# Score chunks of an attention pair issued together, the third one in borrowed PSUM banks

## The chip, the cores and the metric

The kernel runs on one core of a Trainium2 chip. The metric is device microseconds for one execution; lower is better. The engines are TensorE (PE: matmuls, and PEld for its weight loads), VectorE (DVE), ScalarE (ACT), GpSimd (POOL) and SyncE (SP), which issues most DMAs. Each engine takes its instructions in the order in which they were written; they are tied together by semaphores.

## The reference: what is computed

Two stages. First an attention with 4 batches, 8 heads, 768 positions and head size 64, in which a query sees the first 8 keys and the 96 before it, with a bias by distance:

```
scores = scale * q @ k.T                       # per head
keep = is_global | is_local                    # first 8 keys, or 0 <= rel < 96
scores = where(keep, scores - slope[h] * dist, -1e9)
x = softmax(scores) @ v                        # heads side by side: [4, 768, 512]
```

Then a mixer on x, with a low rank product over positions (U: 768x32, V: 32x768) and a feed-forward layer of 512 to 2048 to 512:

```
u = x + (x.T @ U @ V).T
out = u + relu(u @ w_ch1) @ w_ch2
```

## The kernel before, in words

**Pairs.** Work goes by pairs of heads: 16 pairs, `i` from 0 to 15, four to a batch (`NP` is 4, `NPE` is 8). Since the window is narrow, a pair's scores take 1408 columns per head instead of 768 x 6: for each of six key blocks a diagonal piece and, for five of them, a piece for the next block. The columns are made in three chunks, `c` = 0, 1, 2, of 512, 512 and 384 columns per head.

**A chunk** (`scores`, L347). Small matmuls with 64 contraction rows, one head in the upper and one in the lower half of the array: 8 for a full chunk, 6 for the third. From pair 4 on they go to `ps_sc()`, a PSUM tile of two banks (one per head) of which there is a single one. `s_dve` (L399) takes it from there: one VectorE operation on both heads multiplies, adds the bias table and writes the SBUF tile `sp` ("bias step" in what follows). `sp` has one buffer. `st_S` is one chunk and its bias step. When all three chunks are in `sp`, `st_E` makes the exp of one head on ScalarE (L415), first head 0, then head 1, into `ep`.

**Around it.** `st_V(i, hi)` multiplies the exp of one head with v into `ps_ob()`, a single bank, and normalises on VectorE (reciprocal L437, product L451); POOL casts the result to fp16 (`x16`, L454). `st_M1` (L457) is x^T U on PE into the same single bank `ps_ob()`; ScalarE copies it (L467); `st_MT` (L477) transposes that on PE (L480) and VectorE copies it (L481); `st_M3` (L511) multiplies with V into `ps_sc()`, VectorE adds it to x (L522) and POOL casts x again (L525). `st_X` sends it through a DMA transpose to `uT`. `st_K` makes the key tile `kA` of the next pair on ScalarE (L339) and VectorE (L340).

**Feed-forward units.** Meanwhile the feed-forward layer of an earlier batch runs in units. An up unit (L631) is 8 matmuls into one bank `ps_th("hps")`, of which there are three in turn, and a relu on ScalarE (L636) that frees it. Down units (L666 for batch 0, L684 for the others, with sums of halves on VectorE, L555, so that seven products stand for eight) go to `ps_cps`, two banks in turn; VectorE adds each to x (L689).

**What sets the order.** The whole program is written out by hand under `manual_schedule`. The main loop (L804) runs over pairs: iteration `i` makes the scores and exps of pair `i`, the v products of pair `i - 1` and its mixer steps. Between these steps stand nine calls `fill(n)`, each of which issues `n` units (up or down, by a rule in `unit`) and, after each unit, VectorE sums that are due. The number of units at the nine places for pairs 7 to 15 is 1, 1, 1, 2, 1, 1, 1, 1, 1. So the order of one iteration before is:

```
S(i,0) u V(i-1,0) u S(i,1) u V(i-1,1) u u S(i,2) u M1(i-1)
E(i,0) u MT(i-1) K(i+1) u M3(i-1) E(i,1) u X(i-1) u
```

where u is a unit. On PE alone S, V, M1, MT, M3 and u are issued; on ScalarE E, K, the copy after M1 and the relus; on VectorE the bias steps, normalisations, additions and sums.

Of the kernel before, what the change touches and what calls it, by code (L numbers as in the profile page):

```python
# [16 lines left out]
ALU = mybir.AluOpType  # L17
# [3 lines left out]
def kernel(  # L21
# [13 lines left out]
    nc = tc.nc  # L35
# [10 lines left out]
    NP = H // 2  # L46
    NPE = 2 * NP
    qk_scale = 1.0 / math.sqrt(D)
# [5 lines left out]
    slope = [2.0 ** (-8.0 * (h + 1) / H) for h in range(H)]  # L54
# [25 lines left out]
    def ps_sc():  # L80

        return psum.tile([P, 2, 512], FP32, name="sc", tag="sc", bufs=1)

    def ps_ob():
        return psum.tile([P, 512], FP32, name="ob", tag="ob", bufs=1)

    def ps_cps(name):
        return psum.tile([P, 512], FP32, name=name, tag="cps", bufs=2)
# [43 lines left out]
    def load_v(i):  # L132
        b, h0 = i // NP, 2 * (i % NP)
        st = stp.tile([P, 2 * NSB, D], FP32, name="vst", tag="vst", bufs=2)
        nc.sync.dma_start(
            st, v[b, h0:h0 + 2].rearrange("h (n p) d -> p (h n) d", p=P)
        )
        vsts[i] = st
# [27 lines left out]
    def warm(n):  # L166
# [13 lines left out]
        out=relB, in_=relB, compare_op=ALU.is_ge, fill=BIG,  # L180
# [3 lines left out]
        out=relB, in_=relB, compare_op=ALU.is_ge, fill=BIG,  # L184
# [50 lines left out]
    def new_batch(b):  # L235
        xs[b] = xp.tile([P, NSB, DM], FP32, name="x_sb", tag="x_sb", bufs=3)
        tmps[b] = xp.tile([P, DM], FP16, name="tmp16", tag="tmp16", bufs=3)
        uTs[b] = xp.tile([P, NDC, S], FP16, name="uT", tag="uT")
# [76 lines left out]
    def st_P(i):  # L315
        nc.vector.tensor_copy(  # L316
            vas[i][0:NG, 1:].rearrange("p n h d -> p n (h d)"),
            vts[i][0:NG, 0:1].rearrange("p n h d -> p n (h d)").broadcast_to(
                (NG, NSB - 2, 2 * (D + 1))
            ),  # L320
        )
# [22 lines left out]

    sps, eps, later = {}, {}, []

    def scores(i, c, on_pe):  # L347

        kT, kA, qT = kts[i], kas[i], qts[i]
        c0 = 512 * c  # L350
        tot = min(512, W - c0)
        r0 = 256 if c else 0
        both = None if on_pe and (i + c) % 2 else ps_sc()
        scs = [ps_cps("sc") if both is None else both[:, hi] for hi in range(2)]
        if on_pe:
            for hi in range(2):
                nc.tensor.matmul(
                    scs[hi][:, 0:tot], slI[:, 2 * (i % NP) + hi],
                    rel16.rearrange("p a c -> p (a c)")[:, r0:r0 + tot], start=True, stop=False,
                )  # L360
        for kb in (2 * c, 2 * c + 1):
            o = 256 * kb - c0
            for hi in range(2):
                r = slice(hi * D, (hi + 1) * D)
                nc.tensor.matmul(  # L365
                    scs[hi][:, o:o + P], kT[r, kb * P:(kb + 1) * P], qT[r, kb * P:(kb + 1) * P],
                    start=(o == 0 and not on_pe), stop=(o + P == tot),
                )
            if kb < NSB - 1:
                for hi in range(2):  # L370
                    r = slice(hi * D, (hi + 1) * D)
                    nc.tensor.matmul(  # L372
                        scs[hi][:, o + P:o + 2 * P], kA[r, kb], qT[r, (kb + 1) * P:(kb + 2) * P],
                        start=False, stop=(o + 2 * P == tot),
                    )
        return scs, both, c0, tot
# [20 lines left out]
    relfs = (relcat2[:, :, 0:512], relcat2[:, :, 256:768], relcat2[:, :, 256:640])  # L397

    def s_dve(i, got):  # L399
        _, both, c0, tot = got  # L400
        if c0 == 0:
            sps[i] = scp.tile([P, 2, W], FP32, name="sp", tag="sp", bufs=1)
        nc.vector.scalar_tensor_tensor(  # L403
            out=sps[i][:, :, c0:c0 + tot], in0=both[:, :, 0:tot],
            scalar=qk_scale / slope[2 * (i % NP)], in1=relfs[c0 // 512],
            op0=ALU.mult, op1=ALU.add,
        )

    def st_S(i, c):
        s_dve(i, scores(i, c, False))  # L410

    def st_E(i, hi):
        if hi == 0:
            eps[i] = scp.tile([P, 2, W], FP16, name="ep", tag="ep")
        nc.scalar.activation(  # L415
            eps[i][:, hi], sps[i][:, hi], AF.Exp, scale=slope[2 * (i % NP)]
        )
# [59 lines left out]
    def st_MT(i):  # L477
        b, dc = i // NP, i % NP
        tps = ps_ob()
        nc.tensor.matmul(tps[:, 0:P], turn16[i % 2], ident16, start=True, stop=True)  # L480
        nc.vector.tensor_copy(tmps[b][:, dc * P:(dc + 1) * P], tps[:, 0:P])  # L481
# [234 lines left out]
    def fill(n):  # L716
        for _ in range(n):
            unit()
            count[0] += 1
            for _ in range(2 if len(jobs) > 4 else 1):  # L720
                for queue in (jobs, slow):
                    if queue and queue[0][0] < count[0]:
                        queue.popleft()[1]()
                        break

    def unit():
        down = downs_q and not held[0] and not any(place(w) <= place(downs_q[0][1]) for _, w in ups_q)
        room = ups_q and (not downs_q or place(ups_q[0][1]) - place(downs_q[0][1])
                          < (3 if held[0] else 2))
        if down and (ahead[0] > 0 or not room):  # L730
            ahead[0] = 0
            downs_q.popleft()[0]()
        elif room:
            ahead[0] = 1
            ups_q.popleft()[0]()
# [68 lines left out]
    for i in range(NP, NPAIR + 2):  # L804
        b, hp = divmod(i, NP)
        live = i < NPAIR
        units = iter(
            (0, 1, 1, 2, 1, 1, 1, 1, 1) if i == NP
            else (0, 1, 1, 1, 1, 1, 1, 1, 1) if i + 1 < NPE
            else (1, 1, 1, 2, 1, 1, 1, 1, 1)  # L810
        )
        held[0] = i < NP + 3
        if hp == 0 and live and b + 1 < B:
            new_batch(b + 1)
        if live and i > NP:
            st_S(i, 0)
        if NPE <= i + 1 < NPAIR:
            turn(i + 1)
        if i + 1 < NPAIR and i != NP + 2:
            load_v(i + 1)  # L820
        if i + 2 < NPE:
            load_qk(i + 2)
        fill(next(units))
        if NPE + 2 <= i + 2 < NPAIR:
            cast_one(i + 2, 1, nc.scalar)
        if NP < i <= NPAIR:
            st_V(i - 1, 0)
        if i == NP:
            load_w1(2)
        if i + 1 < NPE:  # L830
            st_T(i + 1)
        if i == NP:
            load_w1(3)
        fill(next(units))
        if live:
            st_S(i, 1)
        fill(next(units))
        if NP < i <= NPAIR:
            st_V(i - 1, 1)
        if live:  # L840
            cast_v(i)
            st_A(i)
        if NPE + 2 <= i + 2 < NPAIR:
            cast_one(i + 2, 0, nc.scalar)
        if NPE <= i + 3 < NPAIR and i != NP + 2:
            load_qk(i + 3)
        if i > NP + 1 and (i - 2) % NP == NP - 1:
            queue_ff((i - 2) // NP)
            ahead[0] = 1
        if i == NPAIR + 1:  # L850
            break
        fill(next(units))
        if live:
            st_S(i, 2)
        fill(next(units))
        if i > NP:
            st_M1(i - 1)
        else:
            for xo, o, rb in later:
                nc.vector.tensor_tensor(xo, o, rb, ALU.mult)  # L860
        if i == NP + 1:
            load_w2(0)
            load_w2(1)
        if i + 2 < NPE:
            cast_qk(i + 2, nc.gpsimd)
        if i == NP + 1:
            load_w2(2)
            load_w2(3)
        if live:
            st_E(i, 0)  # L870
            if i < NPE:
                st_P(i)
        fill(next(units))
        if i >= NPE:
            for _ in range(min(2, len(kept))):
                kept.popleft()()
        if i > NP:
            st_MT(i - 1)
        if NPE <= i + 1 < NPAIR:
            st_K(i + 1)  # L880
        fill(next(units))
        if i > NP:
            st_M3(i - 1)
        if live:
            st_E(i, 1)
        fill(next(units))
        if i == NP + 1:
            load_v(i + 2)
            load_qk(i + 4)
        if i > NP:  # L890
            st_X(i - 1)
        if NPE <= i + 2 < NPE + 2:
            cast_qk(i + 2, nc.gpsimd)
        fill(next(units))
# [38 lines left out]
```

## Time and profile before

| what | value |
|---|---|
| median of 3 runs | 232.99 us (231.74 to 235.61) |
| the profiled execution, its own time | 231.74 us |
| its span, first to last instruction | 230.0 us |
| granted TensorE clock | 1.00 |
| instructions | 5877 |
| busy: PE, PEld | 220.7, 171.1 us |
| busy: DVE, ACT, POOL | 161.5, 125.8, 72.3 us |
| bias steps, 36 (L403) | 40.7 us on DVE; 1215 ns for 2 x 512 columns, 944 for 2 x 384 |
| exps, 24 (L415) | 33.1 us on ACT, 1380 ns each |
| first score matmul of pairs 7, 8, ... 15 | 61.02, 73.32, 84.85, 96.42, 107.99, 119.19, 130.38, 142.04, 153.24 us |
| last score matmul of pair 15 starts | 159.2 us |

How to read it: the time is that of an execution with what lies around it; the span is from the first to the last instruction of the program. Busy time on PE is modelled from starts, since matmuls overlap in a pipeline: a matmul of 256 columns is printed with some 270 ns, and eight of them follow each other every 109 ns. The distance of starts therefore says more than the printed lengths. VectorE and ScalarE instructions also overlap slightly: the next one starts some 0.08 us before the printed end of the one before. In the group view, "idle before" is the time for which the engine stood before instructions of that group, and the name behind the arrow is what ended most of it.

### The profile page before, as it was taken

How to read it: one execution, taken by the hardware profiler on the slowest of the kernel's cores; microseconds unless marked ns; L12 is line 12 of the kernel's file. 1: busy time of each engine (PE TensorE's matmuls, PEld its weight loads, DVE VectorE, ACT ScalarE, POOL GpSimd, SP SyncE). 2: the span in 40 equal slices, each digit the busy share in tenths (PEclk: the TensorE clock that was granted, in tenths of full speed). 3: DMA queues.
4: the chain of work that ended last, by engine and by line, in shares of the span. 5: the costliest groups of instructions: out<-in, count | busy, mean ns of one | idle time of the engine just before them, and what ended most of it. 6: DMA issues, size and time to landing. Idle time of an engine off the chain costs nothing.

```text
span 230.0 us, 5877 instructions
## 1 busy us (share of the span) xinstructions
PE 220.7 (96%) x2418; PEld 171.1 (74%) x2420; DVE 161.5 (70%) x337; ACT 125.8 (55%) x196; POOL 72.3 (31%) x115
## 2 busy tenths in 40 slices
PE   7989899999999999999999999999999999999993
PEld 2456568788745445888888878888988888888882
DVE  3799876749577979597989897989764444444452
ACT  6787747786805253968485847292732433333320
POOL 6499708297553323123313131313111000000000
PEclk9999999999999999999999999999999999999999
DMA  6999996979999879897979994951321202010022
GB/s 185 335 283 281 281 291 90 321 135 180 191 163 206 201 180 228 203 239 175 261 202 219 242 200 102 144 158 25 88 69 36 94 0 94 0 67 27 10 84 93
DMA packets 86563, 36.68 MB, mean 160 GB/s; under 512 B 74152, under 2 KB 83592, under 8 KB 86536
## 3 DMA queue, kind: packets, MB, share of 16 engines
q1 hardware_dynamic: 81480, 32.01, 57.5%
q0 software_dynamic: 5056, 4.29, 12.4%
q8 instruction: 19, 0.31, 0.6%
q14 instruction: 8, 0.07, 0.1%
HBM read 27.46 MB, written 6.29 MB: 147 GB/s over the span
## 4 chain that ended last, share of the span: by engine, by line
PE 67%; DVE 15%; DMA 7%; ACT 4%; POOL 2%; issue 1%; SPq 0%; ACTq 0%
PE hps L631 25%; PE cx L684 13%; PE cy L684 10%; PE cps L666 8%; DMA w<-in_moe_w_ch_dram 6%; DVE sp L403 3%; PE sc L365 2%; ACT ep L415 2%; DVE x_sb L451 2%; PE tp L254 2%; PE ob L432 2%; DMA kst<-in_k_dram 2%; PE sc L517 1%; PE ob L428 1%; DVE s L555 1%
## 5 line engine op out<-in xcount | busy, mean ns | idle before, releaser
L631 PE MATMUL hps<-uT,w 128*128 128x256 f16 x756 | 96.0, 273 | 0.0
L636 ACT ACTIVATE htr<-hps 128x512 f16<-128x512 f32 x96 | 56.4, 598 | 58.0 <-PE hps L631 57.9
L631 PEld LDWEIGHTS <-w 128*128 128x128 f16 x756 | 70.5, 98 | 9.9 <-issue 0.2
L403 DVE SCALAR_TENSOR_TENSOR sp<-sc,relcat 128x1024 f32<-128x1024 f32 (+1 forms) x36 | 40.7, 1131 | 9.1 <-ACT ep L415 4.8
L415 ACT ACTIVATE ep<-sp 128x1408 f16<-128x1408 f32 x24 | 33.1, 1380 | 0.7 <-DVE sp L403 0.6
L684 PEld LDWEIGHTS <-htr 128*128 128x128 f16 x288 | 27.5, 98 | 3.6
L454 POOL CAST x<-x_sb 128x384 f16<-128x384 f32 x27 | 14.5, 538 | 49.8 <-DVE x_sb L451 45.7
L689 DVE TENSOR_TENSOR x_sb<-cx,x_sb 128x256 f32<-128x256 f32 x36 | 15.2, 422 | 18.3 <-PE cx L684 17.7
L666 PE MATMUL cps<-w,htr 128*128 128x512 f16 x96 | 24.0, 379 | 0.4 <-DMA w<-in_moe_w_ch_dram 0.4
L525 POOL CAST x<-x_sb 128x768 f16<-128x768 f32 x12 | 11.0, 916 | 40.8 <-DVE x_sb L522 40.8
L684 PEld LDWEIGHTS <-s 128*128 128x128 f16 x216 | 20.2, 98 | 2.9 <-DVE s L555 0.6
L689 DVE TENSOR_TENSOR x_sb<-cy,x_sb 128x256 f32<-128x256 f32 x27 | 11.4, 423 | 12.5 <-PE cy L684 12.3
L365 PEld LDWEIGHTS <-kT 64*128 64x128 f16 x192 | 8.3, 93 | 13.7 <-issue 12.4
L451 DVE TENSOR_TENSOR x_sb<-ob,rcp 128x384 f32<-128x384 f32 x30 | 16.7, 558 | 1.0
L365 PE MATMUL sc<-qT,kT 64*128 64x128 f16 x192 | 16.8, 221 | 0.3 <-DVE x_sb L522 0.2
L432 PE MATMUL ob<-v,ep 128*128 128x65 f16 x192 | 16.4, 193 | 0.0
L432 PEld LDWEIGHTS <-ep 128*128 128x128 f16 x192 | 13.8, 98 | 3.1 <-ACT x L787 0.7
L428 PE MATMUL ob<-vA,ep 128*128 128x65 f16 x160 | 14.5, 194 | 1.2 <-DVE vA L316 1.2
L142 POOL CAST v<-vst 128x768 f16<-128x768 f32 x16 | 14.0, 877 | 2.9 <-DMA vst<-in_v_dram 2.9
L372 PE MATMUL sc<-qT,kA 64*128 64x128 f16 x160 | 14.3, 217 | 0.6 <-DVE kA L290 0.4
L666 PEld LDWEIGHTS <-htr 128*128 128x128 f16 x96 | 8.4, 97 | 8.5 <-issue 0.5
L522 DVE TENSOR_TENSOR x_sb<-sc,x_sb 128x768 f32<-128x768 f32 x12 | 11.5, 956 | 4.6 <-PE sc L517 4.6
(109 smaller groups left out, 315.0 us busy)
## 6 DMA issues: line engine op xcount, KB each, us to landing
qst<-in_q_dram SPq DMA_DIRECT2D x16, 384.0 KB, 4.7
kst<-in_k_dram SPq DMA_DIRECT2D x16, 384.0 KB, 6.1
vst<-in_v_dram SPq DMA_DIRECT2D x16, 384.0 KB, 4.0
out_dram<-x_sb SPq DMA_DIRECT2D x23, 256.0 KB, 3.1
w<-in_moe_w_ch_dram POOLq DMA_DIRECT2D x8, 512.0 KB, 8.1
vA<-v SPq DMA_DIRECT2D x8, 152.3 KB, 3.0
out_dram<-x_sb SPq DMA_DIRECT2D x2, 128.0 KB
uT<-x SPq DMA_TRANSPOSE x12, 3.1
```

The lines of the kernel that those rows point to most:

```text
L365: nc.tensor.matmul(scs[hi][:, o:o + P], kT[r, kb * P:(kb + 1) * P], qT[r, kb * P:(kb + 1) * P], start=(o == 0 and not on_pe), stop=(o + P ...
L403: nc.vector.scalar_tensor_tensor(out=sps[i][:, :, c0:c0 + tot], in0=both[:, :, 0:tot], scalar=qk_scale / slope[2 * (i % NP)], in1=relfs[c0 ...
L415: nc.scalar.activation(eps[i][:, hi], sps[i][:, hi], AF.Exp, scale=slope[2 * (i % NP)])
L428: nc.tensor.matmul(ob[:, qi], ep[:, OF[qi - 1]:OF[qi - 1] + P], vA[:, qi - 1, hi], start=True, stop=False,)
L432: nc.tensor.matmul(ob[:, qi], ep[:, DG[qi]:DG[qi] + P], vt[:, qi, hi], start=(qi == 0), stop=True,)
L451: nc.vector.tensor_tensor(xo, ob[:, :, 0:D], rb, ALU.mult)
L454: nc.gpsimd.tensor_copy(x16, xo)
L631: nc.tensor.matmul(hps[:, k * FT:(k + 1) * FT], w1_16[:, dc, jt * P:(jt + 1) * P], uT[:, dc, ts], start=(dc == 0 and k == 0), stop=(dc == ...
L636: nc.scalar.activation(cell["htr"][:, 2 * jp:2 * jp + 2].rearrange("p j t -> p (j t)"), hps, AF.Relu)
L666: nc.tensor.matmul(cps, htr[:, jc, t * P:(t + 1) * P], w2_16[:, jc], start=(b > 0 and jc == 0), stop=(jc == NJC - 1),)
L684: nc.tensor.matmul(ps, cell[a][:, j], weight(w, j), start=(first and j == 0), stop=(done is not None and j == HJ - 1), skip_group_check=True,)
L689: nc.vector.tensor_tensor(x_sb[:, n, cs], ps, x_sb[:, n, cs], ALU.add)
```

## The change

From pair 7 on (`joined = i >= NPE - 1`):

- The third chunk's matmuls are issued right behind the second's (`st_S12`), where the second stood before.
- The third chunk goes to two banks of `ps_th`, the three that the up units and the transposes of q and k take in turn, instead of the one two-bank tile `ps_sc()`. Since these two banks are separate tiles, its bias step is two operations, one per head, of 128 x 384.
- On VectorE the two bias steps of the third chunk stand first, then that of the second chunk.
- The exp of head 0 stands where the third chunk stood (ahead of a unit and M1); the exp of head 1 stands behind MT and ahead of the next pair's `kA` copy, a unit and M3.

```diff
-    def scores(i, c, on_pe):
+    def scores(i, c, on_pe, apart=False):
...
-        both = None if on_pe and (i + c) % 2 else ps_sc()
-        scs = [ps_cps("sc") if both is None else both[:, hi] for hi in range(2)]
+        both = None if apart or on_pe and (i + c) % 2 else ps_sc()
+        bank = ps_th if apart else ps_cps
+        scs = [bank("sc") if both is None else both[:, hi] for hi in range(2)]
...
     def s_dve(i, got):
-        _, both, c0, tot = got
+        scs, both, c0, tot = got
         if c0 == 0:
             sps[i] = scp.tile([P, 2, W], FP32, name="sp", tag="sp", bufs=1)
+        if both is None:
+            for hi, sc in enumerate(scs):
+                nc.vector.scalar_tensor_tensor(
+                    out=sps[i][:, hi, c0:c0 + tot], in0=sc[:, 0:tot],
+                    scalar=qk_scale / slope[2 * (i % NP)], in1=relfs[c0 // 512][:, hi],
+                    op0=ALU.mult, op1=ALU.add,
+                )
+            return
...
+    def st_S12(i):
+
+        mid = scores(i, 1, False)
+        s_dve(i, scores(i, 2, False, True))
+        s_dve(i, mid)
...
         fill(next(units))
+        joined = i >= NPE - 1
         if live:
-            st_S(i, 1)
+            st_S12(i) if joined else st_S(i, 1)
         fill(next(units))
...
         fill(next(units))
-        if live:
+        if live and joined:
+            st_E(i, 0)
+        elif live:
             st_S(i, 2)
         fill(next(units))
         if i > NP:
...
-        if live:
+        if live and not joined:
             st_E(i, 0)
-            if i < NPE:
-                st_P(i)
+        if live and i < NPE:
+            st_P(i)
         fill(next(units))
...
         if i > NP:
             st_MT(i - 1)
+        if live and joined:
+            st_E(i, 1)
         if NPE <= i + 1 < NPAIR:
             st_K(i + 1)
         fill(next(units))
         if i > NP:
             st_M3(i - 1)
-        if live:
+        if live and not joined:
             st_E(i, 1)
```

The order of one iteration with the change, for pairs 7 to 15:

```
S(i,0) u V(i-1,0) u S(i,1) S(i,2) u V(i-1,1) u u E(i,0) u M1(i-1)
u MT(i-1) E(i,1) K(i+1) u M3(i-1) u X(i-1) u
```

## The prediction

> **What bounds the kernel now.** The page first: TensorE (PE) is busy for 96% of the span at full clock, so time can only come from its gaps.
>
> ```profile
> PE 220.7 (96%) x2418; PEld 171.1 (74%) x2420; DVE 161.5 (70%) x337; ACT 125.8 (55%) x196; POOL 72.3 (31%) x115
> ```
>
> Then the stage table. The edit acts from pair 7 (first chunk at 61.0 us) to pair 15 (last chunk at 159.2 us); columns are the stretch, its length, and busy time of PE, PEld, DVE, ACT, POOL.
>
> ```profile
> 108.00:130.00 22.00, 22.00 (x273) 18.62 (x273) 19.21 (x40) 14.89 (x23) 5.08 (x8) 1.00 0.99 227
> 164.00:230.00 66.00, 62.13 (x592) 55.39 (x589) 31.12 (x81) 20.80 (x36) 2.93 (x4) 1.00 0.16 54
> ```
>
> VectorE (DVE) is 87% busy in the first of them: second tightest. After 164 us nothing of the edit is left, and the chain of waits runs on PE alone; what PE gains or loses before then moves the end one for one.
>
> Third, PE's timeline in pair 12.
>
> ```profile
> 121.70 0.23 PE L365 MATMUL sc<-qT,kT 64*128 64x128 f16 x2
> 121.88 0.22 PE L372 MATMUL sc<-qT,kA 64*128 64x128 f16 x2
> 122.03 1.05 PE L631 MATMUL hps<-uT,w 128*128 128x256 f16 x8
> ...
> 124.12 1.04 PE L631 MATMUL hps<-uT,w 128*128 128x256 f16 x8
> 125.09 0.23 PE L365 MATMUL sc<-qT,kT 64*128 64x128 f16 x2
> 125.22 0.22 PE L365 MATMUL sc<-qT,kT 64*128 64x128 f16 x2
> 125.37 0.61 PE L684 MATMUL cx<-slI,htr 128*128 128x256 f16 x4
> ...
> 126.25 0.30 PE L463 MATMUL ob<-u,x 128*128 128x32 f16 x6
> ```
>
> Score matmuls come in pairs 0.06 us apart (121.70 to 121.88 is three steps). Going in, 124.12 + 8 x 0.109 = 124.99, but the third chunk starts at 125.09: 0.10 lost. Coming out, its last pair starts at 125.22 and the next matmul at 125.37 instead of 125.28: 0.09 lost. Every chunk from 96 us on shows these two sums; they are most of PE's gaps. Real waits between 86 and 164 us are few: 0.38 (pair 10, at 105.8), 0.45 (pair 13, at 137.4), 0.20 (at 90.4).
>
> Fourth, DVE and POOL in the same pair: who feeds L463 (U^T x, called M1 here).
>
> ```profile
> 121.73 0.56 DVE L451 TENSOR_TENSOR x_sb<-ob,rcp 128x384 f32<-128x384 f32 x1
> 123.05 1.21 DVE L403 SCALAR_TENSOR_TENSOR sp<-sc,relcat 128x1024 f32<-128x1024 f32 x1
> 124.40 0.56 DVE L451 TENSOR_TENSOR x_sb<-ob,rcp 128x384 f32<-128x384 f32 x1
> 125.48 0.96 DVE L403 SCALAR_TENSOR_TENSOR sp<-sc,relcat 128x768 f32<-128x768 f32 x1 [0.18 <-PE sc L365]
> 125.03 0.51 POOL L454 CAST x<-x_sb 128x384 f16<-128x384 f32 x1 [2.17 <-DVE x_sb L451]
> ```
>
> M1 reads what POOL casts from the second normalisation (L451 at 124.40). The cast ends at 125.54, M1 starts at 126.25: 0.7 us of cover. The third bias step (125.48) stands behind it today.
>
> Fifth, ScalarE (ACT) in pair 14: L467 copies M1's result for the transpose L480 (MT) and stands ahead of the exp.
>
> ```profile
> 149.31 0.60 ACT L636 ACTIVATE htr<-hps 128x512 f16<-128x512 f32 x1 [0.66 <-PE hps L631]
> 149.80 0.18 ACT L467 CAST zw<-ob 128x32 f16<-128x32 f32 x1
> 150.02 1.38 ACT L415 ACTIVATE ep<-sp 128x1408 f16<-128x1408 f32 x1
> ...
> 150.13 0.22 PE L480 MATMUL ob<-ident,zw 128*128 128x128 f16 x1
> ```
>
> **The change, part by part.**
>
> *Third chunk beside the second (9 pairs).* One way in and one out go: 0.10 + 0.09 = 0.19 us per pair, 1.7 us in all, on the bounding engine. No matmul is added.
>
> *Third chunk in two up banks.* Three banks serve the up units. I followed them pair by pair: the two taken had their relu (L636) done at least 0.4 us before, and the unit after next gets one back once the first third-chunk step is done, 0.5 to 0.7 us before it starts. Cost nothing; without that cover, the step's remainder, at most 0.5 us per pair.
>
> *Bias steps: two of 128x384, then the 1024-column one.* No row has 128x384 of this operation. From 1215 ns at 1024 columns and 944 at 768 a column costs 1.06 ns, so 384 take 0.54 us; the nearest row of that width (L451, also from PSUM) has 0.56. Steps follow each other 0.08 us before the printed end, so a step advances DVE by 0.46 (1.14 for 1024 columns). Two against one of 0.87 is +0.05 us per pair, not on the path itself. Bounds: 0 (split free) to 0.1 (0.56 each, less overlap); I take 0.05.
>
> *What they are moved past.* This is the price. The order of the built program puts all three ahead of the reciprocal and normalisation of the second head, so these come 0.92 us later, more where the burst must wait for the third chunk's matmuls (0.19 later than the second's). Behind them queue POOL's cast, M1, the L689 additions and the s sums (L555). M1 itself comes 0.19 earlier on PE.
>
> Pair 12: burst at 123.05 (DVE was busy to then), + 0.46 + 0.46 + 1.14 = 125.11; reciprocal 0.22, normalisation 0.56, to POOL 0.07, cast 0.51, to PE 0.05: M1 can start at 126.52. Before: 126.25. So a wait of 0.46 eats the 0.19: +0.27.
>
> The others go by the same sum, with 0.33 for each addition or sum that the new order puts between burst and reciprocal (0.60 for the weight difference). The burst starts when DVE is free for the second step as before, or 0.58 after the second chunk's first matmul, when the third's result is there. Burst start; M1 possible; M1 before; net:
> - 7: 64.35; 67.8; 69.02; no wait, -0.19
> - 8: 77.29; 81.09; 80.54; +0.55 (DVE is behind already)
> - 9: 88.20; 92.27; 92.29; M1 waits 0.17, see exp below
> - 10: 100.11; 103.91; 103.48; +0.43 (its old 0.38 wait at 105.8 ends on a chain from M1 and stays)
> - 11: 111.10; 115.23; 115.06; +0.17
> - 12: +0.27
> - 14: 145.10; 148.90; 149.10; -0.19 here, see exp
> - 15: 157.03; 160.50; 160.30; +0.20
>
> Pair 13's PE stands on the s sum before its cx product, not on M1. Burst from 133.50 to 135.56, then 0.33 + 0.22 + 0.48 + 0.33 + 0.33 + 0.42 = 137.67; before it ended at 137.41. That is +0.26, and +0.78 if the last sum takes 0.94 as it did before; I take +0.40.
>
> The row first: that sum ran 136.47 to 137.41 while POOL cast v (136.11 to 137.14), others of its shape take 0.42. The Trainium skill ("SBUF — State Buffer", section "SBUF: two separate sides") says VectorE and GpSimd share a port pair as an exclusive lock, taken by VectorE operations with two SBUF inputs, and not shared in time. By that rule the sum would wait for the cast again in the new order, and the total below would be 0.4 us higher.
>
> *Exps earlier.* The first exp now stands ahead of the fourth unit's relu and of M1's copy L467; the second ahead of the kA copy (0.68). Where that unit is an up, the copy waits for exp and relu. Pair 14: relu of the third stretch's up from 148.24, exp from 148.73 (+1.29), relu to 150.51, copy to 150.69, MT at 150.74 against 150.13: +0.61. Pair 9: relu 91.24, exp 91.73, relu 93.02, copy 93.51, MT 93.73 against 93.31: +0.42. Elsewhere the copy is ready in time. The kA copy lands by 130.2 in pair 12, needed at 130.6; if it were not, 0.7 us at most. What earlier exps free: the next first bias step waited for an exp in pairs 10 and 11 (0.33 and 0.78 of DVE idle); pair 10's burst starts 0.35 earlier, which is in the list, and pair 11's next finds its matmuls only then. No DMA is issued elsewhere: the SP and POOL orders are unchanged.
>
> **Sum.** -0.19 + 0.55 + 0.42 + 0.43 + 0.17 + 0.27 + 0.40 + 0.61 + 0.20 = +2.9 us. The profiled execution took 231.74 us (230.0 span and 1.7 around it), so 234.6. That execution is the fastest of three; on the median of 232.99 the same step would be 235.8.
>
> **Rivals.**
> *The saving stands alone.* All waits stay covered: 231.74 - 1.7 = 230.0. For it: PE hardly waits today and M1 has 0.7 us of cover. Against: the burst is longer than that cover in six pairs.
> *Exp and burst decide in every pair.* One mechanism: the copy for MT sits behind an exp that cannot start before the three-step burst ends, so MT is late in each pair, as worked out for pair 14. At its 0.61 in all nine: +5.5, so 237.2: slower by over 2%. It decides from 0.52 net per pair (4.7/9). For it: DVE at 87% has no room to catch up, and ACT's order is fixed. Against: in five pairs no relu stands between exp and copy.
> *The two chunks don't join.* If the third chunk waits for its up banks, PE stands in the middle and the 1.7 is spent again: 234.6 + 1.7 = 236.3. Pair 13, with two ups ahead, comes nearest; its bank is free at 132.39, needed at 133.1.
>
> **How the numbers follow.** Forecast 0.42, saving alone 0.20, exp and burst 0.33, no joining 0.05. Within 2% is about what a measurement of this kernel can tell from no change (runs before spread from 231.74 to 235.61). Slower by over 2%: 0.33 and a part of the last, 0.35; faster by over 2% needs 4.7 us where PE's gaps hardly hold that: 0.03; the rest, 0.62. The range goes from 230.3, just above the saving alone, to 238.0, which holds 237.2 and 0.8 for port waits and the higher median.
>
> **What would show it.** Right: score groups of 14 matmuls with one way in and out; DVE's three L403-type steps adjoining; a PE wait of 0.2 to 0.6 ahead of M1 in pairs 8, 10, 11, 12, 15 and ahead of MT in 9 and 14; the stage after pair 15 unchanged in length. Wrong: M1 without waits, or waits ahead of the third chunk's own matmuls or of ups (banks), or waits in pair 7.

## The result, and the profile after

The changed kernel took 235.03 us (median of 6 runs, 234.14 to 235.59) against 232.47 us for the kernel before (6 runs, 229.99 to 235.61): ratio 1.0143, 95% interval 1.0106 to 1.0181. The ratio is taken over executions in the fast state alone, so it is not the quotient of the two medians. The changed kernel is slower, clear of noise, though within 2%. The profiled execution has a span of 233.6 us, 3.6 more than before's.

The page's line of engines:

```profile
PE 219.5 (94%) x2418; PEld 170.6 (73%) x2420; DVE 161.0 (69%) x346; ACT 126.1 (54%) x196; POOL 72.2 (31%) x115
```

Two stages with the same work in both kernels. The first runs from the first M3 matmul in pair 10's iteration to that in pair 12's; this is the kernel before:

```profile
105.81:128.21 22.40, 22.39 (x275) 18.79 (x275) 18.94 (x39) 15.29 (x24) 5.64 (x8) 1.00 0.96 221
```

And the changed kernel, with the tail, all that follows pair 15, as the second stage:

```profile
106.80:130.03 23.23, 22.48 (x275) 18.79 (x275) 18.37 (x41) 14.30 (x23) 5.84 (x8) 1.00 0.92 204
167.70:233.62 65.92, 62.13 (x592) 55.37 (x589) 31.13 (x81) 20.63 (x36) 2.92 (x4) 1.00 0.16 54
```

PE does the same work (275 matmuls) and now stands still for 0.75 us of the first stage. The tail is 65.9 us; before it is 66.0. So the loss lies between pair 7 and pair 15.

PE's timeline in pair 12. The two chunks stand together:

```profile
123.43 0.23 PE L366 MATMUL sc<-qT,kT 64*128 64x128 f16 x2
...
123.61 0.22 PE L373 MATMUL sc<-qT,kA 64*128 64x128 f16 x2
123.67 0.22 PE L366 MATMUL sc<-qT,kT 64*128 64x128 f16 x2
...
123.78 0.22 PE L366 MATMUL sc<-qT,kT 64*128 64x128 f16 x2
123.93 1.05 PE L646 MATMUL hps<-uT,w 128*128 128x256 f16 x8
...
127.77 0.31 PE L478 MATMUL ob<-u,x 128*128 128x32 f16 x6
```

From the second chunk's last pair (123.61) to the third's first (123.67) is the ordinary 0.06: one way in and one out are gone. Behind this, DVE and POOL in the same pair:

```profile
124.30 1.01 DVE L406 SCALAR_TENSOR_TENSOR sp<-sc,relcat 128x384 f32<-128x384 f32 x2
125.23 1.21 DVE L412 SCALAR_TENSOR_TENSOR sp<-sc,relcat 128x1024 f32<-128x1024 f32 x1
126.36 0.18 DVE L452 RECIPROCAL rcp<-ob 128x6 f32<-128x6 f32 x1
126.58 0.56 DVE L466 TENSOR_TENSOR x_sb<-ob,rcp 128x384 f32<-128x384 f32 x1
127.20 0.51 POOL L469 CAST x<-x_sb 128x384 f16<-128x384 f32 x1 [3.10 <-DVE x_sb L466]
```

The burst takes 2.06 us (124.30 to 126.36), the cast ends at 127.71, and M1 starts at 127.77, right behind it. M1's 0.7 us of cover is used up; in this pair PE does not wait for it, since an earlier wait (for vA, below) had already made PE late.

What PE waited for (in total, times, longest); the first five rows that touch pairs 7 to 15:

```profile
PE ob L478 <- POOL x L469: 2.1, 5, 0.8
PE cx L699 <- DVE s L570: 1.6, 1, 1.6
...
PE cps L681 <- DMA w<-in_moe_w_ch_dram: 0.9, 1, 0.9
...
PE ob L495 <- ACT zw L482: 0.8, 2, 0.5
...
PE ob L443 <- DMA vA<-v: 0.3, 1, 0.3
```

L478 is M1, L495 is MT; vA is a copy of v in another layout, which two DMAs make. These totals count from the printed end of the matmul ahead. By distance of starts, pairs 8 to 15 have 6.8 us of waits, against 1.0 before: M1 0.99, 0.36, 0.68, 0.53 and 0.41 (pairs 8 to 11 and 15), MT 0.41, 0.29 and 0.70 (9, 12, 14), the s sum 1.75 (13), vA 0.42 (12), M3 0.28 (10). 5.8 more, less eight times the 0.19 that the join saves, is +4.3.

The second row is pair 13:

```profile
138.75 0.60 DVE L570 TENSOR_TENSOR s<-htr 128x512 f16<-128x512 f16 x1
139.38 0.93 DVE L570 TENSOR_TENSOR s<-s,htr 128x512 f16<-128x512 f16 x1
139.02 1.03 POOL L142 CAST v<-vst 128x768 f16<-128x768 f32 x1
140.38 0.61 PE L699 MATMUL cx<-t,s 128*128 128x256 f16 x4 [1.58 <-DVE s L570]
```

The same sum and cast before the change:

```profile
136.47 0.94 DVE L555 TENSOR_TENSOR s<-s,htr 128x512 f16<-128x512 f16 x1
136.11 1.03 POOL L142 CAST v<-vst 128x768 f16<-128x768 f32 x1
137.46 0.61 PE L684 MATMUL cx<-t,s 128*128 128x256 f16 x4 [0.28 <-DVE s L555]
```

And pair 14, ACT and the MT that waits for it:

```profile
151.13 0.60 ACT L651 ACTIVATE htr<-hps 128x512 f16<-128x512 f32 x1 [1.49 <-PE hps L646]
151.63 1.37 ACT L430 ACTIVATE ep<-sp 128x1408 f16<-128x1408 f32 x1
152.89 0.59 ACT L651 ACTIVATE htr<-hps 128x512 f16<-128x512 f32 x1
153.37 0.19 ACT L482 CAST zw<-ob 128x32 f16<-128x32 f32 x1
153.61 0.23 PE L495 MATMUL ob<-ident,zw 128*128 128x128 f16 x1 [0.54 <-ACT zw L482]
```

### The profile page after: what moved, and what is told of

It reads as the page before. It is cut to its first block, busy times and chain, and to the rows that moved or that the text cites. A ratio compares the mean times of both kernels' runs of the same rounds, so it can differ in the third digit from the quotient of the medians.

```text
span 233.6 us, 5877 instructions
## 1 busy us (share of the span) xinstructions
PE 219.5 (94%) x2418; PEld 170.6 (73%) x2420; DVE 161.0 (69%) x346; ACT 126.1 (54%) x196; POOL 72.2 (31%) x115
## 4 chain that ended last, share of the span: by engine, by line
PE 53%; DVE 21%; DMA 10%; ACT 7%; POOL 4%; issue 4%; SPq 0%; DVEq 0%; POOLq 0%
PE hps L646 19%; PE cx L699 10%; PE cy L699 8%; DMA w<-in_moe_w_ch_dram 6%; PE cps L681 6%; DVE sp L412 5%; ACT ep L430 3%; DVE x_sb L466 3%; DVE s L570 3%; DVE sp L406 2%; DMA vA<-v 2%; PE tp L254 2%; PE sc L366 2%; DMA kst<-in_k_dram 2%; DVE x_sb L704 2%
## 5 line engine op out<-in xcount | busy, mean ns | idle before, releaser
L412 DVE SCALAR_TENSOR_TENSOR sp<-sc,relcat 128x1024 f32<-128x1024 f32 (+1 forms) x27 | 32.1, 1188 | 7.6 <-ACT ep L430 4.0
L704 DVE TENSOR_TENSOR x_sb<-cy,x_sb 128x256 f32<-128x256 f32 x27 | 11.4, 422 | 12.5 <-PE cy L699 12.3
L366 PE MATMUL sc<-qT,kT 64*128 64x128 f16 x192 | 15.7, 221 | 0.3 <-DVE x_sb L537 0.2
L129 ACT CAST k<-kst 128x768 f16<-128x768 f32 x6 | 5.0, 832 | 17.7 <-DMA kst<-in_k_dram 17.7
```

Of the source, the lines that this page charges most:

```text
L366: nc.tensor.matmul(scs[hi][:, o:o + P], kT[r, kb * P:(kb + 1) * P], qT[r, kb * P:(kb + 1) * P], start=(o == 0 and not on_pe), stop=(o + P ...
L412: nc.vector.scalar_tensor_tensor(out=sps[i][:, :, c0:c0 + tot], in0=both[:, :, 0:tot], scalar=qk_scale / slope[2 * (i % NP)], in1=relfs[c0 ...
L704: nc.vector.tensor_tensor(x_sb[:, n, cs], ps, x_sb[:, n, cs], ALU.add)
```

## The experiments

Executions differ before pair 7: by 0.9 us between the two profiles above. The profiles of two experiments, the banks alone and the late join, reach pair 7 4.9 and 3.2 us late, mostly since PE waited 3.8 and 2.5 us for a cast of k whose load was late; in both, the granted clock was 0.93 from 20 to 45 us and 1.00 in the stretch compared below. Pair 7 itself contains a wait for a load of weights, which is none to 1.7 us from profile to profile. So besides the ratio I compare one stretch of the profiles: from the first M3 matmul (L517 of before) in pair 7's iteration to that in pair 15's. It is 91.31 us before (70.95 to 162.26) and 95.57 after (70.38 to 165.95): +4.3, as added up above. There is one profile of each kernel; where a pair's matmuls stand in the same order in two of them and have no wait, its distance from M3 to M3 agrees to 0.02 us.

Two theories were at stake for that sum. *Burst*: the bias steps put ahead of the second normalisation make M1 and the s sums late. *Exps*: standing ahead of M1's copy they make MT late. The rival to both was the borrowed banks.

**The banks alone.** The third chunk stays in its old place, with bias steps and exps as before, but in two up banks. Against the kernel before, and besides the change's own edit of `scores` and `s_dve`, that is:

```diff
-    def st_S(i, c):
-        s_dve(i, scores(i, c, False))
+    def st_S(i, c, apart=False):
+        s_dve(i, scores(i, c, False, apart))
...
-            st_S(i, 2)
+            st_S(i, 2, joined)
```

> One part alone: the third chunk goes to two up banks with two bias steps of 128x384, but its matmuls, its bias steps and the exps stand where they stood before. Burst theory (the cost is the bias steps put ahead of the second normalisation): the banks themselves cost nothing, so before's time within 0.5 us (ratio 0.998 to 1.003), PE waits ahead of M1 and MT as in before (none over 0.1 us). Bank theory (two of three up banks borrowed makes up units or the third chunk wait): ratio 1.005 or more, with PE waits ahead of L631-type matmuls or of the third chunk.

Ratio 1.0051 (1.0012 to 1.0091); the stretch 92.73 us, +1.4. PE's waits:

```profile
PE hps L646 <- ACT htr L651: 0.8, 2, 0.4
PE hps L646 <- DVE sp L406: 0.5, 1, 0.5
```

My expectation failed: there the banks do cost, 0.6 us each in pairs 9, 11 and 14. In 9 and 14 the third chunk takes the two free banks, and the next up must have the one whose relu has just begun. In 11 the next up waits for the third chunk's own first bias step, which stands behind a sum of 0.98 us on VectorE. In the changed kernel no up and no third chunk waits in pairs 7 to 15, so the 1.4 us belong to this placing, not to the change.

**The exps alone put back.** From here on the changes shown are against the changed kernel.

```diff
-        if live and joined:
-            st_E(i, 0)
-        elif live:
+        if live and not joined:
             st_S(i, 2)
...
-        if live and not joined:
+        if live:
             st_E(i, 0)
...
-        if live and joined:
-            st_E(i, 1)
...
-        if live and not joined:
+        if live:
             st_E(i, 1)
```

So the first exp stands behind M1 and the second behind M3.

> The changed kernel with the exps where they stood before (first behind M1, second behind M3); join, banks and bias order stay. Burst theory: M1 waits stay (pairs 8 to 12 and 15, about 3 us with the s-sum wait of pair 13), the MT waits of pairs 9, 12 and 14 go (0.41 + 0.29 + 0.70 us), so about 1.2 us faster than the changed kernel: ratio to before 1.007 to 1.011. Exp theory (the exps ahead of M1's copy are the main cost): ratio 1.000 or below.

Ratio 1.0097 (1.0058 to 1.0136); the stretch 94.13 us, 1.4 less than the changed kernel. The MT waits are gone, the M1 and s-sum waits stay:

```profile
PE ob L478 <- POOL x L469: 2.3, 6, 0.7
PE cx L699 <- DVE s L570: 1.6, 1, 1.6
```

M1 now waits in pair 12 too (0.40), where vA came in time. So the exps cost 1.4 us, a third of the loss.

**The bias steps alone moved back**, behind the second normalisation; exps early:

```diff
-        s_dve(i, scores(i, 2, False, True))
+        third = scores(i, 2, False, True)
         s_dve(i, mid)
+        return third
...
-            st_S12(i) if joined else st_S(i, 1)
+            third = st_S12(i) if joined else st_S(i, 1)
...
             st_V(i - 1, 1)
+        if live and joined:
+            s_dve(i, third)
```

> The changed kernel with the third chunk's two bias steps moved behind the second head's normalisation on VectorE (the second chunk's step stays ahead of it); the matmuls stay joined, the exps stay where the change put them. Burst theory: the waits ahead of M1 go in all pairs and the saved 1.7 us of the join show, less waits of up units whose bank is freed some 1 us later (0 to 0.5 us in the pairs with two ups between, so 0 to 2 us) and less the MT waits, since the first exp now starts later: ratio to before 0.997 to 1.008, M1 waits under 0.2 us each. If M1 waits stay as they are in the changed kernel (0.36 to 0.99 us), the burst theory is wrong.

Ratio 1.0045 (1.0003 to 1.0088); the stretch 93.05 us, 2.5 less than the changed kernel. No M1 wait is left, as expected; MT waits instead (2.4 us in five pairs), since the exp starts later:

```profile
PE ob L496 <- ACT zw L483: 1.2, 2, 0.6
PE cx L700 <- DVE s L571: 1.0, 2, 0.8
```

**Both put back**: what remains of the change is the join and the banks.

> Joined matmuls in borrowed banks, with the third chunk's bias steps behind the second normalisation and the exps where they stood before: what is left of the change is the join and the banks. If burst and exps together are the whole cost, the MT waits seen with the bias steps moved back alone (0.74, 0.26, 0.30, 0.79 and 0.30 us in pairs 9, 11, 12, 14, 15: 2.4 us) go too, and it is about 2 us faster than that kernel: ratio to before 0.993 to 1.000. If something else of the change costs (banks, s sums), it stays at 1.003 or above.

Ratio 0.9986 (0.9957 to 1.0015); the stretch 91.29 us, before's to 0.02. Burst and exps together are worth the whole loss: 4.3 us go with them (2.5 + 1.4 one at a time). The join's saving does show, pair by pair. From M3 of pair 11's iteration to that of pair 12's the kernel before takes 11.20 us:

```profile
117.01 0.50 PE L517 MATMUL sc<-tmp,v16w 128*128 128x128 f16 x6
...
128.21 0.50 PE L517 MATMUL sc<-tmp,v16w 128*128 128x128 f16 x6
```

This one takes 10.99:

```profile
116.61 0.50 PE L533 MATMUL sc<-tmp,v16w 128*128 128x128 f16 x6
...
127.60 0.50 PE L533 MATMUL sc<-tmp,v16w 128*128 128x128 f16 x6
```

Pairs 8, 11, 14 and 15 gain the same 0.2 us, and pair 9 gains 0.4. New waits in two pairs take it all back: pair 10 is 1.1 us longer, pair 13 (the s sum) 0.3. The largest wait is an up in pair 10, 1.1 us by distance of starts, printed as 0.95:

```profile
99.40 0.83 ACT L129 CAST k<-kst 128x768 f16<-128x768 f32 x1 [1.95 <-DMA kst<-in_k_dram]
100.14 0.59 ACT L652 ACTIVATE htr<-hps 128x512 f16<-128x512 f32 x1
100.78 0.81 PE L647 MATMUL hps<-uT,w 128*128 128x256 f16 x6 [0.95 <-ACT htr L652]
```

ACT stands 1.95 us before the cast of k until its load lands; the relu that would free the bank is queued behind it. The third chunk's bias steps start only at 101.32, so the two other banks are still taken. In the kernel before, ACT waits 1.14 us at the same cast and no up waits behind it. The Trainium skill says of the order ("PSUM — Partial Sum Buffer", section "Engine vs sequencer instructions") that the queues of ScalarE, VectorE and GpSimd are strict FIFO; the trace agrees in this row, and in MT's wait behind the exp.

**The burst made longer.** In the changed kernel each of the third chunk's bias steps is issued twice:

```diff
-        s_dve(i, scores(i, 2, False, True))
+        third = scores(i, 2, False, True)
+        s_dve(i, third)
+        s_dve(i, third)
         s_dve(i, mid)
```

> The changed kernel with the third chunk's two bias steps each issued twice (the same result is written again): the burst ahead of the second normalisation is 0.92 us longer, nothing else changes. Burst theory: each wait that hangs on the burst grows by about 0.9 us: ahead of M1 in pairs 8 to 12 and 15 (0.99, 0.36, 0.68, 0.53, about 0.3, 0.41 before), the s-sum wait of pair 13, and pairs 14 and 7 use up what slack they have; some 7 us more than the changed kernel in all, ratio to before 1.035 to 1.050. Theory that VectorE has room and the waits come from elsewhere: under 2 us more, 1.022 or below.

Ratio 1.0525 (1.0453 to 1.0597, two runs), above the 1.050 that I expected at most; the stretch 102.85 us, 7.3 more than the changed kernel for 0.92 more in each of its eight pairs. M1 waits:

```profile
PE ob L480 <- POOL x L471: 5.2, 6, 1.4
```

Not all of the 7.3 us is the burst. PE's waits in the stretch grow from 6.8 to 12.5 us, by 5.7. The rest goes with the clock, which fell soon behind the longest of these waits (2.1 us in pair 13), so that PE's busy time in the stretch grew from 90.6 to 92.4 us. The column ahead of the last two is the granted clock:

```profile
143.00:147.00 4.00, 1.86 (x21) 1.44 (x21) 3.22 (x8) 1.87 (x3) 1.48 (x2) 1.00 0.74 165
147.00:151.00 4.00, 4.00 (x27) 3.09 (x25) 2.23 (x6) 2.44 (x3) 0.00 (x0) 0.57 0.15 40
```

So some three quarters of the dose (5.7 of 7.4 us) come through as waits. They reach PE in every pair: outside pairs 13 and 14, where the clock was low, each is 0.5 to 0.9 us longer than in the changed kernel. In pairs 10 and 11 it is not M1 that waits longer but an up, for its bank (0.9 and 1.0 us).

**The other order in the burst**, the second chunk's step first, then the third's two.

> The changed kernel with the three bias steps in the other order: the second chunk's ahead of the third's two. Burst theory: the normalisation still comes behind all three, so M1, MT and s-sum waits stay as in the changed kernel (sum within 0.5 us), ratio 1.011 to 1.018. Bank theory (third first is needed to hand the up banks back in time): up units wait for banks that are freed 1.1 us later, 0.3 us or more in the pairs with an up directly behind the second head's product (pairs 10 and 11), so up to 1 us slower than the changed kernel.

Ratio 1.0147 (1.0106 to 1.0187); the stretch 95.08 us, 0.5 less than the changed kernel. An up waits 0.4 us behind the second product in pair 11, as the bank theory said, but other waits are shorter. "Bias steps first" makes no difference that these runs can tell: what counts is what stands behind all three.

**Both chunks where the third stood**, with exps as before the change, so that nothing is put ahead of the normalisation:

```diff
-            st_S12(i) if joined else st_S(i, 1)
+            if not joined:
+                st_S(i, 1)
...
-        if live and joined:
-            st_E(i, 0)
-        elif live:
-            st_S(i, 2)
+        if live:
+            st_S12(i) if joined else st_S(i, 2)
```

> Second and third chunk stand together where the third stood (behind the second head's product and two units), third in up banks with its bias steps first, exps where they stood before. Nothing is put ahead of the second normalisation any more. Burst theory: no M1 waits (under 0.1 us), the join's 1.7 us are saved, but the burst now stands ahead of the copy behind MT: waits ahead of M3 of 0 to 0.5 us per pair; ratio to before 0.992 to 1.006. Theory that joining itself costs (banks, row mode): 1.01 as in the changed kernel.

Ratio 1.0134 (1.004 to 1.0228, few runs), not the 1.006 at most that I expected; the stretch 93.86 us, +2.6 on before. M1 waits vanish as expected; M3 waits for the copy behind MT, up to 1.3 us where I had expected 0.5 at most:

```profile
PE sc L532 <- DVE tmp L496: 2.9, 6, 1.3
```

Ups wait another 1.2 us in pairs 9 to 11 and 14, and a v product 0.4 in pair 12. The theory that joining itself costs gave such a ratio too; the kernel with both put back excludes it. In both places where the burst was put whole, 2.06 us on DVE make something late.

**The cast of v earlier.** In the changed kernel from pair 8 on, POOL casts v ahead of the second product's result:

```diff
+            if live and i >= NPE:
+                cast_v(i)
+                st_A(i)
             st_V(i - 1, 1)
-        if live:
+        if live and i < NPE:
             cast_v(i)
             st_A(i)
```

> The changed kernel with the cast of v (and the two copies that make vA from it) issued ahead of the second head's product instead of behind it, from pair 8 on, so that POOL casts v before and not after the second normalisation's result. If the s-sum wait of pair 13 (1.75 us) is partly the sum being slowed beside that cast, and the wait for vA in pair 12 (0.42 us) its late start, both shrink, by 0.6 and 0.4 us: about 1 us faster than the changed kernel, ratio 1.008 to 1.012. If the sum is slow for another reason, 1.014 stays.

Ratio 1.0164 (1.0111 to 1.0216, few runs), which can't be told from the changed kernel's and is not the 1.008 to 1.012 that I expected; the stretch is 94.38 us, 1.2 less. So the waits below are shown, and a gain in time is not. The vA wait of pair 12 is gone (M1 waits 0.41 there instead). Pair 13:

```profile
138.96 0.60 DVE L570 TENSOR_TENSOR s<-htr 128x512 f16<-128x512 f16 x1
139.59 0.42 DVE L570 TENSOR_TENSOR s<-s,htr 128x512 f16<-128x512 f16 x1
135.70 0.84 POOL L142 CAST v<-vst 128x768 f16<-128x768 f32 x1
```

Away from the cast the sum takes 0.42 instead of 0.93, and PE's wait falls from 1.75 to 1.24 us, by distance of starts.

**Towards a better kernel.** Bias steps and exps back, and v cast early:

> The kernel with bias steps and exps moved back, and the cast of v ahead of the second head's product as well. The candidate to beat both kernels: the join's 1.7 us less waits for up banks (about 0.4 us in pair 10) and what remains of the s-sum waits: ratio to before 0.990 to 0.998. If casting v earlier delays POOL's cast for M1, M1 waits show and it is no faster than the same kernel without.

Median 230.62 us against 231.35 of before, ratio 0.9977 (0.9941 to 1.0013); the stretch 90.80 us, 0.5 less than before. No M1 wait appears. An up in pair 10 (0.8 us, now behind the third chunk's bias step) and pair 13's s sum (0.9 us) remain.

The same, but the first head's third bias step ahead of the second chunk's, so that one bank is free early (against the last kernel):

```diff
+        s_dve(i, third, (0,))
         s_dve(i, mid)
         return third
...
-            s_dve(i, third)
+            s_dve(i, third, (1,))
```

> The fastest kernel so far (bias steps behind the normalisation, exps back, v cast early) with the first head's third bias step put back ahead of the second chunk's, so that one borrowed bank is free early; the second head's stays behind the normalisation. The up unit of pair 10 that waited for a bank there (0.8 us) should not wait; the burst ahead of the normalisation is 0.46 us longer, so by the burst theory M1 waits come back only where its slack was under 0.5 us: pair 8 (about 0.3 us) and pair 10 (about 0.2 us). Net 0 to 0.5 us faster: ratio to before 0.994 to 0.999. If the burst theory is wrong on slack, M1 waits of 0.4 us in all pairs, ratio above 1.005.

Median 230.85 us against 231.81, ratio 0.9971 (0.9942 to 1.0001); the stretch 90.79 us. Pair 10's up no longer waits; its M1 waits 0.5 us instead (0.2 expected), pair 8's does not (0.3 expected), pair 13's sum stays late by 1.05. The two versions can't be told apart, and neither beats before by more than the interval; both beat the changed kernel by some 1.7%, ratio against ratio.

## Why the prediction was right, point by point

Forecast +2.9 us on the profiled execution (231.74 to 234.6, or 235.8 on the median); measured 235.03, which is +2.6 between the medians, and +3.6 between the two spans. Between M3 of pair 6's iteration and that of pair 15's the profiles differ by +4.6; the lead of 0.9 us that the second execution had before pair 7 makes it +3.6 in the spans. 0.55 of the 4.6 is pair 7's wait for a load of weights (1.11 us against 0.56), which differs from profile to profile; without it the change costs +4.0 in these profiles. So direction and mechanism were right and the terms too small by about 1.2 us, 0.7 of it in pair 13. That the forecast time came as close to 235.03 as 0.4 us is in part luck, as executions of the kernel before spread over more than 5 us. By pair (distance of M3 starts, after less before; forecast in brackets): 7 +0.34 (-0.19), 8 +0.79 (+0.55), 9 +0.38 (+0.42), 10 +0.38 (+0.43), 11 +0.33 (+0.17), 12 +0.50 (+0.27), 13 +1.09 (+0.40), 14 +0.58 (+0.61), 15 +0.20 (+0.20).

- *What bounds the kernel*: held. The tail's length did not move, and PE's losses before it are the difference.
- *The join*: held. Chunks stand 0.06 us apart, every other entry and exit still costs 0.10 and 0.09, and with burst and exps put back the pairs without a new wait are 0.2 us shorter.
- *Up banks at no cost*: held where the change puts the chunk; no up and no third chunk waits in it. The cover is thin: with the chunk in its old place (1.4 us), or with the bias steps later (1.1 us in one pair), ups wait for them.
- *Two steps for one*: held; two advance DVE by 0.93 (124.30 to 125.23) where I had 0.92.
- *Burst ahead of the normalisation*: held, and it is the main cost (2.5 us by taking it away, 5.7 us more of waits by adding 0.92 per pair). M1 waits in 8, 9, 10, 11 and 15, where forecast, but 0.36 to 0.99 us where I had named 0.2 to 0.6. Pair 8 was undersized: the cast took 0.63 and not 0.51, and the burst began 0.1 later. Pair 12, the pair that I worked through, shows no M1 wait here: the wait for vA ahead of it took its place. Where vA came in time, with the exps back or v cast early, M1 waits 0.40 and 0.41 there, against 0.46 in the working.
- *Exps ahead of the copy*: held (1.4 us). Pairs 9 and 14 came as worked out; pair 12 (0.29) I had called ready in time.
- *Pair 13*: the right wait, the wrong size. PE waited 1.75 us there, against 0.45 before. The sum took 0.93, as before the change, and not the 0.56 that is implied by the +0.40 that I chose between +0.26 and +0.78; the sum ahead of it took 0.60, not 0.33. By the Trainium skill's rule of the port pair that VectorE and GpSimd share ("SBUF — State Buffer", "SBUF: two separate sides") the total would have been 3.3. The trace agrees: sum and cast together last from 139.02 to 140.31, 1.29 us, where they take 0.42 and 0.84 apart, and moving the cast away gave the sum its 0.42 back.
- *Missed*: the cast of v stands behind the late one on POOL, and vA's transfer is issued behind that (117.33, before the change 116.30). It came 0.42 us late for pair 12's first product, a term that I had at nothing: I wrote that no DMA is issued elsewhere, which holds for the order and not for the time. The later issue alone does not explain the wait, since pair 12 itself began 1.3 us later; the transfer also took 4.8 us to land, against 2.7. Casting v early removed the wait (2.7 again); why the transfer took longer stays open.

Of the rivals, the saving alone is excluded by the waits. That exp and burst decide in every pair was too much for this kernel (pair 7 has slack at M1, and MT is late in three pairs only); with a burst 0.92 longer, every pair is longer. The chunks did join.

## What to carry to other kernels

Before operations are moved up on an engine that is not the bound, follow what they overtake to the next instruction of the bounding engine, and compare the delay with the cover that the trace shows there: in pair 12 here, 0.92 us against 0.7. A saving of 0.19 us per pair on the bounding engine was lost to a chain through DVE and POOL that had idle time on average (DVE is 69% busy over the span). Casts and transfers queued behind the delayed one count as well. And a saving is best looked for pair by pair: in the total, two new waits hid it.

## What the runs showed of the hardware

A VectorE sum of two SBUF tiles (128x512, fp16) takes 0.42 us alone and 0.93 beside a POOL cast of 128x768; moving the cast away restored 0.42. A ScalarE wait for a load passed on through the engine's queue: 1.95 us of waiting for k became 1.1 us of TensorE waiting for a PSUM bank. And in the kernel with the longer burst the granted clock was 0.57 from 147 to 151 us, soon behind TensorE's wait of 2.1 us; that the wait brought it about, no run here shows.
